# A decode-attention kernel: ScalarE's last seven turns as a hardware loop, exponentials in two halves, last output weights one head a transfer

## The chip, the cores and the metric

One core of a Trainium2 chip runs the kernel. The metric is the device time of one execution in microseconds (us). A program on one core shows no second, slower die to compare with; every run below was judged "fast" by its own spread. Every run was timed in turns with the kernel before on the same chip; the runs were on several chips.

## The reference, cut to what matters

```python
# twice, for A (all 8192 keys) and B (the last 2048 keys): B=4, one query token, 32 heads, 8 kv heads, Dh=128
q = (x @ wq).reshape(B, 1, 32, 128)            # D = 512
scores = einsum("bhqd,bhkd->bhqk", q, k) * 128 ** -0.5
o = einsum("bhqk,bhkd->bhqd", softmax(scores), v)
out = o.reshape(B, 1, 4096) @ wo               # A and B side by side
```

Everything is bfloat16. K and V are read once: 184.56 MB from HBM with the weights.

## The kernel before: the parts that matter here

The work is cut into 20 units (4 of B, then 16 of A: one batch entry, two kv heads), two units to a turn. In unit u, TensorE transposes K of u into PSUM, and VectorE (even groups) and ScalarE (odd groups) copy it to SBUF. TensorE forms the scores, VectorE subtracts the maximum, and ScalarE takes the exponential. One unit later TensorE multiplies by V. K and V have two buffers each, filled by loads that SyncE issues.

```python
def op(eng, fn, waits=(), inc=None, bump=None):
    ...                          # an op with a turn number is emitted once, in a hardware loop
    t = turn[0] if eng == "pe" or (eng == "dve" and turn[0] is not None and turn[0] >= T0P) else None   # T0P = 3

def act_exp(u, h0=0, h1=2):      # h0, h1: which halves of the 1024 columns
    a, b = h0 * NTH * C, h1 * NTH * C
    def fn(act):
        return act.activation(out=PT[:, u % 2, a:b], in_=Dt[:, a:b], func=ACTF.Exp, scale=scale)
    return dict(eng="act", fn=fn, waits=[("sub", u, h1 - 1)] + ([("otr", u - 2)] if u >= 2 else []), ...)

# in kv_load(kind, u): what a load of unit u waits for (the buffer of unit u-2)
w = [("T", tjob_idx[(u - 2, NJ - 1)])] if kind == "K" else [("otr", u - 2)]   # last transpose; scaled output
...                                                                          # SyncE's order: K(u), then V(u-1)

WCH = [3, 2, 2, 1]               # last output weights: heads per transfer
for i, n in enumerate(WCH):      # the last projection, two halves of the columns in two PSUM banks
    for hq in range(h0, h0 + n):
        for hf in range(2):
            ...                  # matmul, waits for ("WL", i)
```

TensorE's ten turns and VectorE's last seven are already hardware loops. A loop of this kernel subtracts what its semaphores gained in each turn (`emit_loop` in the kernel), so no other engine may wait on those semaphores while the loop runs.

Of the kernel before, what the change touches and what calls it, by code (L numbers as in the profile page):

```python
# [14 lines left out]
def bass_concat_heads__gqa_block_cached__sliding_block_cached__decode_kernel(  # L15
# [25 lines left out]
    C = 2 * REP  # L41
    NJ = NT // 8
# [21 lines left out]
    L = NU - 1  # L64
    NTURN = NU // 2
    T0P = 3
# [4 lines left out]
    with ExitStack() as es:  # L71
# [8 lines left out]
        def sm(name):  # L80
# [5 lines left out]
        Wo_sb = sb("Wo_sb", [128, 2, REP, D], BF16)  # L86
# [33 lines left out]
        KTB = [ps("KT%d" % i, 512) for i in range(NBK)]  # L120
        OTB = ps("OT", 512)

        names = ["k0", "k1", "kh", "v0", "v1", "vl0", "vl1", "vl2", "vl3", "wl0", "wl1", "wl2", "wl3", "x0", "x1", "w0", "w1", "wo",
                 "out0", "out1", "out2", "Tq", "Td", "Ta", "S", "PV", "Ed", "Ea", "Eq", "max", "sub", "sum", "rcp", "exp", "otr", "os", "otp",
                 "ocp", "Ef", "fin0", "fin1", "ar1", "SM", "maxc", "pset", "setup", "pm0", "pm1", "oc", "ocB", "mk0", "mk", "mka", "perm", "rq"]
        sems = {n: sm("s_" + n) for n in names}
# [3 lines left out]
        jobs = []  # L130
        bank_last = {}
        follow = {}
        tjob_idx, qp_idx, xt_idx, perm_idx, ot_idx, ol_idx, opj_idx = {}, {}, {}, {}, {}, {}, {}
# [26 lines left out]
        plan = {e: [] for e in ("sp", "pe", "act", "dve", "pool")}  # L160
        turn = [None]

        def op(eng, fn, waits=(), inc=None, bump=None):
            waits = list(waits)
            if not (eng == "pe" and turn[0] is not None):
                waits = [w for w in waits if w is not None]
            t = turn[0] if eng == "pe" or (eng == "dve" and turn[0] is not None and turn[0] >= T0P) else None
            plan[eng].append(dict(fn=fn, waits=waits, inc=inc, turn=t, bump=bump))

        def add(d):  # L170
            op(d["eng"], d["fn"], waits=d["waits"], inc=d["inc"])
# [284 lines left out]
        def act_exp(u, h0=0, h1=2):  # L456
            a, b = h0 * NTH * C, h1 * NTH * C

            def fn(act):
                return act.activation(out=PT[:, u % 2, a:b], in_=Dt[:, a:b], func=ACTF.Exp, scale=scale)  # L460
            return dict(eng="act", fn=fn, waits=[("sub", u, h1 - 1)] + ([("otr", u - 2)] if u >= 2 else []),
                        inc=("exp", u) if h1 == 2 else ("exp", u, h0))

        def dve_sum(u):
            S, n = nseg(u), ncol(u)
# [99 lines left out]
        def dma(dst, src):  # L565
            def fn(e):
                return e.dma_start(out=dst, in_=src)  # L567
            return fn
# [33 lines left out]
        for u in range(NU):  # L602
            turn[0] = tn = u // 2
            odd = u % 2 == 0
            ev = {}
            extra = {}
            at = -1

            def anchored(d):
                extra.setdefault(at, []).append(d)  # L610
            for tok in TOK:
                if tok[0] == "T":
                    ev[tok[1]] = pe_T(u, tok[1])
                    if tok[1] % 2 == 0:
                        at = tok[1]
                elif tok[0] == "S":
                    pe_S(u, tok[1])
                elif tok[0] == "X":
                    if u % 2 == 1:
                        ev["opj"] = pe_job_OPJ(tn)  # L620
                    else:
                        pe_filler(NFILL)
                elif tok[0] == "SM":
                    pe_SM(u - 1)
                else:
                    pe_PV(u - 1, tok[1], waits=[("V", u - 1) if u >= 1 else None] if tok[1] == 0 else [])
                if odd and tok in AFTER:
                    kind = AFTER[tok][0]
                    anchored({"OT": pe_job_OT, "OL": pe_job_OL}[kind](tn))

            if u % 2 == 0 and tn:
                follow[opj_idx[tn - 1]] = tjob_idx[(u, 0)]
            for k in range(0, NJ, 2):
                add(ev[k])
                if k == 10:
                    add(dve_max(u, 0))
                for d in extra.get(k, []):
                    add(d)
            add(dve_max(u, 1))
            if units[u]["P"] == 0:  # L640
                add(dve_maxc(u))
            add(dve_addmask(u))
            if u >= 1:
                add(dve_sum(u - 1))
                add(dve_rcp(u - 1))
            add(dve_submask(u))
            add(dve_sub(u, 0))
            add(dve_sub(u, 1))
            if u >= 1:
                add_norm(u - 1)  # L650
            if u % 2 == 1:
                add(ev["opj"])

            for k in range(1, NJ, 2):
                add(ev[k])
            if u == L:
                add(act_exp(u, 0, 1))
                add(act_exp(u, 1, 2))
            else:
                add(act_exp(u))  # L660

            if u % 2 == 0:
                if tn:
                    op("pool", None, waits=[("ocp", tn - 1)])
                if tn - 1 == T0P + NSEG - 1:
                    op("pool", lambda pool: pool.tensor_copy(out=osb[:, 1, :], in_=oacc[:, :]), inc=("ocB", 0))
                    op("pool", lambda pool: pool.memset(oacc[:, :], 0.0), waits=[("ocB", 0)], inc=("ocB", 1))
                add(pool_otp(tn))
            if u + 1 < NU:
                add(pool_rq(u + 1))  # L670
            add(pool_ar1(u))
            if u >= 1 and units[u - 1]["P"] == 0:
                add(pool_oc(u - 1))
# [14 lines left out]
        for c in range(NC):  # L688
            w = [("VL", vch_of[c])]
# [4 lines left out]
                op("pe", pe_seed, waits=[("ocp", NTURN - 1)])  # L694
            pe_PV(L, c, bank=KTB[0], waits=w)
        add_norm(L, bank=KTB[0])
        WCH = [3, 2, 2, 1]
        h0 = 0
        for i, n in enumerate(WCH):
            for hq in range(h0, h0 + n):  # L700
                for hf in range(2):
                    def lfn(pe, hq=hq, hf=hf):
                        return pe.matmul(out=halves[hf], lhsT=OT_sb[:, 0, NSEG - 1, hq, :], rhs=Wl_sb[:, hq, hf * H2:(hf + 1) * H2],
                                         start=False, stop=(hq == C - 1))
                    op("pe", lfn, waits=[("WL", i), ("otr", L), ("oc", L - 1)], inc=("fin", hf) if hq == C - 1 else None)
            h0 += n
# [4 lines left out]
        def kv_load(kind, u):  # L711
# [6 lines left out]
            if un["P"] == 1:  # L718
                for q in range(NSEG):
                    base = cache[un["b"], 2 * q, SK - W:SK, :]  # L720
                    src = bass.AP(tensor=base.tensor, offset=base.offset, ap=[[TS * DH, 64], [SK * DH, 2], [1, TS * DH]])
                    if kind == "K":
                        w = [("T", tjob_idx[(u - 2, 4 * q + 3)])] if u >= 2 else []
                    else:
                        w = [("otr", u - 2)] if u >= 2 else [("T", tjob_idx[(1, 1)])] if u else [("T", qp_idx[(1, NQP - 1)])]
                    op("sp", dma(buf[:, slot, q * TS:(q + 1) * TS, :], src), waits=w, inc=(kind if q == NSEG - 1 else kind + "h", u, q))
                return
            base = cache[un["b"], 2 * un["gp"], :, :]
            w = [("T", tjob_idx[(u - 2, NJ - 1)])] if kind == "K" else [("otr", u - 2)]
            if kind == "V" and u == L:  # L730
                c0 = 0
                for i, n in enumerate(VCH):
                    t0, t1 = c0 * TC, (c0 + n) * TC
                    src = bass.AP(tensor=base.tensor, offset=base.offset + t0 * DH, ap=[[NT * DH, 128], [1, (t1 - t0) * DH]])
# [17 lines left out]
        for u in range(1, NU + 1):  # L752
            if u < NU:
                kv_load("K", u)
            kv_load("V", u - 1)
            tn = u // 2
            if u % 2 == 0 and tn in pieces:
                P, q = pieces[tn]
                src = WO[P][q * C * DH:(q + 1) * C * DH, :].rearrange("(g p r) n -> p g (r n)", p=128, r=REP)
                op("sp", dma(Wo_sb[:, :, :, :].rearrange("p g r n -> p g (r n)"), src), waits=[("T", tjob_idx[(u, 1)])], inc=("wo", tn))  # L760
            if u == 16:
                op("sp", dma(out[:, 0, D:2 * D], osb[:, 1, :]), waits=[("ocB", 0)], inc=("out", 1))
        h0 = 0
# [31 lines left out]
        def value(key):  # L795
            return values[full(key)]

        def emit(eng_name, eng):
            waited = {}
            for o in plan[eng_name]:  # L800
                for w in o["waits"]:
                    sem, val, _ = value(w)
                    if waited.get(sem.name, 0) >= val:
                        continue
                    eng.wait_ge(sem, val)
                    waited[sem.name] = val
                if o["fn"] is None:
                    continue
                ins = o["fn"](eng)
                if o["inc"] is not None:  # L810
                    sem, val, amt = values[o["inc"]]
                    ins.then_inc(sem, amt)
# [8 lines left out]
        def emit_loop(name, pe, engine):  # L821
# [22 lines left out]
            strides, by_name = {}, {}  # L844
# [27 lines left out]
                    o["w"] = [value(w)[:2] for w in o["waits"]]  # L872
            top0 = {n: max(v for o in turns[0] for s, v in o["w"] if s.name == n) for n in by_name}
            for e in plan:
                assert e == name or not any(value(w)[0].name in by_name for o in plan[e] for w in o["waits"] if w is not None)
            run(ops[:at[0]])
            for n, sem in by_name.items():
                assert strides[n] > 0
# [16 lines left out]

        @block.scalar
        def _(act):
            emit("act", act)

        @block.vector  # L900
        def _(dve):
# [33 lines left out]
```

## Time and profile before

| | kernel before |
|---|---|
| time | 441.33 us median of 3 (441.18 to 441.64) |
| DMA, queue q1 | 98.9% of 16 engines' span, 184.56 MB |
| TensorE / VectorE / ScalarE busy | 83% / 48% / 42% |
| rate from 120 to 400 us | 429 to 431 GB/s |

The page of the kernel before: the span, the busy times, the DMA queues with their packets, megabytes and share of 16 engines, and the chain of waits.

```profile
span 439.6 us, 15816 instructions
PE 366.2 (83%) x7312; PEld 338.0 (77%) x7312; DVE 210.1 (48%) x462; ACT 186.4 (42%) x184; POOL 27.8 (6%) x84
q1 hardware_dynamic: 13088, 184.56, 98.9%
q8 instruction: 8, 0.13, 0.1%
q14 instruction: 6, 0.05, 0.0%
DMA 49%; PE 37%; PEld 8%; issue 3%; SPq 1%; PEldq 0%; DVE 0%; ACT 0%
```

The queue of loads is busy all the time. ScalarE has next to no part in the chain of waits (0% as rounded). q8 and q14 carry the instructions themselves (the page calls both "instruction").

ScalarE's two groups, from the page's costliest groups (busy time, mean of one in ns, then idle time before them and what ended most of it):

```profile
L287 ACT ACTIVATE KT_sb<-KT 128x1024 bf16<-128x1024 bf16 x160 | 163.2, 1024 | 130.6 <-PE KT L278 130.6
L460 ACT ACTIVATE PT<-Dt 128x1024 bf16<-128x1024 f32 (+1 forms) x21 | 21.3, 1017 | 91.8 <-DVE Dt L449 91.8
```

ScalarE waits 222 us in these two groups.

SyncE's queue in the timeline of the kernel before (start, duration, what is issued). K and V come 6.1 us apart in one unit and together in the other:

```profile
187.13 0.34 SPq L567 DMA_DIRECT2D K_sb<-in_A_k_cache_dram  x1
187.58 0.37 SPq L567 DMA_DIRECT2D V_sb<-in_A_v_cache_dram  x1
196.47 0.33 SPq L567 DMA_DIRECT2D K_sb<-in_A_k_cache_dram  x1
202.55 0.33 SPq L567 DMA_DIRECT2D V_sb<-in_A_v_cache_dram  x1
229.16 0.38 SPq L567 DMA_DIRECT2D Wo_sb<-in_B_wo_dram  x1
229.71 0.34 SPq L567 DMA_DIRECT2D K_sb<-in_A_k_cache_dram  x1
```

The last projection in the timeline of the kernel before, some of its 16 matmuls and what follows:

```profile
435.14 0.27 PE L703 MATMUL SA<-Wl_sb,OT_sb 128*4 128x256 bf16 x1
435.77 0.27 PE L703 MATMUL KT<-Wl_sb,OT_sb 128*4 128x256 bf16 x1 [0.36 <-issue]
437.08 0.27 PE L703 MATMUL KT<-Wl_sb,OT_sb 128*4 128x256 bf16 x1
437.28 0.41 DVE L707 CAST osb<-SA 4x256 bf16<-4x256 f32 x1 [2.48 <-PE SA L703]
437.39 0.37 ACT L708 ACTIVATE osb<-KT 4x256 bf16<-4x256 f32 x1 [10.84 <-PE KT L703]
437.79 0.27 ACTq L567 DMA_DIRECT2D out_dram<-osb  x1
```

Matmuls of this kind start 0.11 us apart. Between the third and the fourth there are 0.63 us.

The trace also records 16 landings of every transfer of 128 partitions, without naming an engine. I take each for one of the 16 DMA engines that the page counts; 16 packets of q1 are in flight for 91% of the time from 60 to 400 us. The tables in plain fences in this text are worked out from such records, and from those of single packets. Times are from the span's start:

```
kernel before, transfer landed (its slowest engine)   slowest - second   - median   - first
K, 142.6 us                                                0.04 us       0.27 us    2.13 us
V, 216.7 us                                                0.96          1.22       3.10
V, 423.9 us                                                0.53          1.26       2.77
last weights, 436.51 us                                    0.46          1.10       2.45
```

The engines do not keep step: from 153 to 434 us the slowest and the fastest are 2.7 to 3.1 us apart. They do not even out either: the slowest stays 0.94 to 1.00 us behind the second from 153 to 382 us, and 0.4 to 0.6 us from 392 us to the end. The last weights are complete only when the slowest has landed, at 436.51 us, 1.10 us after the median.

### The profile page before, as it was taken

To read this page: it belongs to the slowest core of one execution; us is meant where nothing else is said; L and a number is where in the kernel's file an instruction comes from. 1 tells how busy PE (TensorE), PEld (TensorE's weight loads), DVE (VectorE), ACT (ScalarE), POOL (GpSimd) and SP (SyncE) were. 2 spreads that over 40 slices of the span, in tenths; PEclk is the share of its full clock that TensorE was granted. 3 is DMA by queue.
4 is the path that set the end of the run, shared out by engine and by line. 5 is a ranking of instruction groups with operands and counts; after the bars stand their busy time and mean duration, and the time that the engine had idled before them with its cause. 6 is when DMAs were issued, how large, how long until landed. Compare 5 with 4: busy or idle time off the path is not lost.

```text
span 439.6 us, 15816 instructions
## 1 busy us (share of the span) xinstructions
PE 366.2 (83%) x7312; PEld 338.0 (77%) x7312; DVE 210.1 (48%) x462; ACT 186.4 (42%) x184; POOL 27.8 (6%) x84
## 2 busy tenths in 40 slices
PE   0158998998997949895989698969878896989986
PEld 0158897997996949795979688968878795979965
DVE  0034455654663634463446346625643563556641
ACT  1004473473562615370635253434534361635630
POOL 6100000000000000000000000000100000000000
PEclk9999999999999988998899799969997999899999
DMA  8999999999999999999999999999999999999995
GB/s 338 427 413 421 418 417 421 423 441 409 444 429 436 418 438 429 429 427 429 432 438 420 433 444 422 437 432 429 413 446 435 429 430 429 432 427 411 447 403 211
DMA packets 13190, 184.77 MB, mean 420 GB/s; under 512 B 1348, under 2 KB 2424, under 8 KB 4472
## 3 DMA queue, kind: packets, MB, share of 16 engines
q1 hardware_dynamic: 13088, 184.56, 98.9%
q8 instruction: 8, 0.13, 0.1%
q14 instruction: 6, 0.05, 0.0%
q0 software_dynamic: 64, 0.02, 0.0%
q10 hardware_dynamic: 24, 0.01, 0.0%
HBM read 184.56 MB, written 0.01 MB: 420 GB/s over the span
## 4 chain that ended last, share of the span: by engine, by line
DMA 49%; PE 37%; PEld 8%; issue 3%; SPq 1%; PEldq 0%; DVE 0%; ACT 0%
DMA K_sb<-in_A_k_cache_dram 37%; PE KT L278 21%; DMA K_sb<-in_B_k_cache_dram 7%; PE OT L325 6%; DMA Wl_sb<-in_A_wo_dram 5%; PEld KT L278 3%; PE SA L309 3%; PE SB L309 3%; PE KT L387 2%; PEld OT L325 1%; SPq L567 1%; PEld SA L309 1%; PEld SB L309 1%; PE SA L337 1%; PE KT L261 0%
## 5 line engine op out<-in xcount | busy, mean ns | idle before, releaser
L278 PE MATMUL KT<-identf,K_sb 128*128 128x128 f32 x1280 | 208.4, 297 | 45.3 <-DMA K_sb<-in_A_k_cache_dram 32.9
L287 ACT ACTIVATE KT_sb<-KT 128x1024 bf16<-128x1024 bf16 x160 | 163.2, 1024 | 130.6 <-PE KT L278 130.6
L278 PEld LDWEIGHTS KT<-identf,K_sb 128*128 128x128 f32 x1280 | 147.6, 149 | 50.8 <-DMA K_sb<-in_A_k_cache_dram 34.1
L286 DVE COPY KT_sb<-KT 128x512 int32<-128x512 int32 x160 | 110.5, 690 | 121.8 <-PE KT L278 120.4
L325 PE MATMUL OT<-PT,V_sb 128*128 128x64 bf16 x2560 | 78.1, 193 | 2.1 <-DMA V_sb<-in_A_v_cache_dram 1.2
L325 PEld LDWEIGHTS OT<-PT,V_sb 128*128 128x128 bf16 x2560 | 75.9, 98 | 2.3 <-DMA V_sb<-in_A_v_cache_dram 1.3
L460 ACT ACTIVATE PT<-Dt 128x1024 bf16<-128x1024 f32 (+1 forms) x21 | 21.3, 1017 | 91.8 <-DVE Dt L449 91.8
L309 PEld LDWEIGHTS SA<-RQc,KT_sb 128*128 128x128 bf16 x1280 | 57.2, 98 | 2.5
L309 PEld LDWEIGHTS SB<-RQc,KT_sb 128*128 128x128 bf16 x1280 | 50.5, 97 | 7.9 <-issue 4.4
L309 PE MATMUL SA<-RQc,KT_sb 128*128 128x16 bf16 x1280 | 56.5, 170 | 0.0
L309 PE MATMUL SB<-RQc,KT_sb 128*128 128x16 bf16 x1280 | 52.8, 170 | 0.0
L411 DVE TENSOR_REDUCE M<-SB 128x8 f32<-128x512 f32 (+1 forms) x20 | 13.8, 692 | 50.3 <-PE SB L309 50.3
L432 POOL PARTITION_ALL_REDUCE MB<-M1m x20 | 7.7, 387 | 335.7 <-DVE M1m L425 335.7
L387 PE MATMUL KT<-Wo_sb,OL 128*4 128x512 bf16 x80 | 18.9, 379 | 0.0
L197 PE MATMUL KT<-ident,x_sb 4*128 4x4 bf16 x8 | 0.6, 170 | 19.5 <-POOL identf L529 19.5
L197 PEld LDWEIGHTS KT<-ident,x_sb 4*128 4x128 bf16 x8 | 0.4, 113 | 19.6 <-issue 19.6
L449 DVE TENSOR_TENSOR Dt<-SA,MBm 128x512 f32<-128x512 f32 x20 | 13.8, 691 | 0.7
L411 DVE TENSOR_REDUCE M<-SA 128x8 f32<-128x512 f32 (+1 forms) x20 | 13.6, 681 | 0.0
L449 DVE TENSOR_TENSOR Dt<-SB,MBm 128x512 f32<-128x512 f32 x20 | 13.6, 681 | 0.0
L337 PE MATMUL SA<-PT,onesb 128*128 128x64 bf16 x336 | 13.2, 192 | 0.0
L387 PEld LDWEIGHTS KT<-Wo_sb,OL 128*4 128x4 bf16 x80 | 6.0, 84 | 8.1
L337 PEld LDWEIGHTS SA<-PT,onesb 128*128 128x128 bf16 x336 | 11.1, 97 | 0.0
(72 smaller groups left out, 125.4 us busy)
## 6 DMA issues: line engine op xcount, KB each, us to landing
K_sb<-in_A_k_cache_dram SPq DMA_DIRECT2D x15, 4096.0 KB, 24.5
V_sb<-in_A_v_cache_dram SPq DMA_DIRECT2D x15, 4096.0 KB, 29.5
K_sb<-in_B_k_cache_dram SPq DMA_DIRECT2D x16, 1024.0 KB, 22.1
V_sb<-in_B_v_cache_dram SPq DMA_DIRECT2D x16, 1024.0 KB, 19.0
V_sb<-in_B_wq_dram SPq DMA_DIRECT2D x1, 4096.0 KB, 12.3
V_sb<-in_A_wq_dram SPq DMA_DIRECT2D x1, 4096.0 KB, 21.7
Wo_sb<-in_B_wo_dram SPq DMA_DIRECT2D x4, 1024.0 KB, 10.2
K_sb<-in_A_k_cache_dram SPq DMA_DIRECT2D x2, 2048.0 KB, 17.3
```

The source lines that it names most:

```text
L278: ins = pe.transpose(out=bkf[:, pi * 128:(pi + 1) * 128], in_=K_sbf[:, slot, t0:t0 + 2, :].rearrange("p t d -> p (t d)"), identity=identf[ ...
L286: return e.tensor_copy(out=KT_sb.bitcast(I32)[:, tj % NKT, :], in_=bkf.bitcast(I32)[:, :])
L287: return e.activation(out=KT_sb[:, tj % NKT, :], in_=bk[:, :], func=ACTF.Copy)
L309: ins = pe.matmul(out=stb[:, t % NTH * C:(t % NTH + 2) * C], lhsT=ktv[:, pi, :, e], rhs=RQc[:, u % 2, t // TS, e, :], start=(e == 0), stop ...
L325: ins = pe.matmul(out=otb[:, s * NW:s * NW + w], lhsT=V_sb[:, slot, t, :], rhs=PT[:, slot, t * C:t * C + w], start=(j == 0), stop=(j == n ...
L337: ins = pe.matmul(out=SA[u % 2][:, s * NW:(s + 1) * NW], lhsT=onesb[:, :], rhs=PT[:, u % 2, c0:c0 + NW], start=(i == 0), stop=(i == n - 1))
L387: ins = pe.matmul(out=bk[0:Bn, 0:D], lhsT=OL[:, i // REP, i % REP, :], rhs=Wo_sb[:, i // REP, i % REP, :], start=(i == 0), stop=(i == C - 1))
L411: return dve.tensor_reduce(out=M1[:, h * n:(h + 1) * n].rearrange("p (s h) -> p s h", h=C), in_=bank[:, :].rearrange("p (s j h) -> p s h j ...
L432: return pool.partition_all_reduce(MB[:, 0:n], M1m[:, 0:n], channels=128, reduce_op=ReduceOp.max)
L449: return dve.tensor_tensor(out=Dt[:, h * NTH * C:(h + 1) * NTH * C].rearrange("p (s j h) -> p s j h", s=Sh, h=C), in0=bank[:, :].rearrange ...
L460: return act.activation(out=PT[:, u % 2, a:b], in_=Dt[:, a:b], func=ACTF.Exp, scale=scale)
L567: return e.dma_start(out=dst, in_=src)
```

## The change

The intent: ScalarE's program becomes a loop as the others' are (fewer instructions to load), the exponential of the first half starts before the second half is subtracted, and the last projection starts with one head's weights. Since a loop's semaphores may not be waited on by others, the loads of K and of the output weights get waits on VectorE's results instead of on the transposes that ScalarE copies. The diff, with only the list of semaphore names left out:

```diff
-            t = turn[0] if eng == "pe" or (eng == "dve" and turn[0] is not None and turn[0] >= T0P) else None
+            t = turn[0] if eng == "pe" or (eng in ("dve", "act") and turn[0] is not None and turn[0] >= T0P) else None
@@ act_exp
-            return dict(eng="act", fn=fn, waits=[("sub", u, h1 - 1)] + ([("otr", u - 2)] if u >= 2 else []),
-                        inc=("exp", u) if h1 == 2 else ("exp", u, h0))
+            return dict(eng="act", fn=fn, waits=[("sub", u, h1 - 1)], inc=("exp", u) if h1 == 2 else ("exp", u, h0))
@@ each unit
-            if u == L:
-                add(act_exp(u, 0, 1))
-                add(act_exp(u, 1, 2))
-            else:
-                add(act_exp(u))
+            add(act_exp(u, 0, 1))
+            add(act_exp(u, 1, 2))
@@ last projection
-        WCH = [3, 2, 2, 1]
+        WCH = [1] * C
-                for hf in range(2):
+                for hf in (1, 0):
@@ kv_load
-            w = [("T", tjob_idx[(u - 2, NJ - 1)])] if kind == "K" else [("otr", u - 2)]
+            w = [("otr", u - 2)] if kind == "V" else [("otr", u - 3)] if u >= 2 * T0P else [("T", tjob_idx[(u - 2, NJ - 1)])]
@@ output weights of the earlier pieces
-                op("sp", dma(Wo_sb...), waits=[("T", tjob_idx[(u, 1)])], inc=("wo", tn))
+                op("sp", dma(Wo_sb...), waits=[("ocp", tn - 1)], inc=("wo", tn))
@@ emit_loop: waits of turns before the loop are allowed
-                assert e == name or not any(value(w)[0].name in by_name for o in plan[e] for w in o["waits"] if w is not None)
+                assert e == name or not any(value(w)[0].name in by_name for o in plan[e] for w in o["waits"] if w is not None
+                                                  and not (name == "act" and w[0] == "T" and (jobs[w[1]]["turn"] or 0) < T0P))
@@ block.scalar
-            emit("act", act)
+            emit_loop("act", act, mybir.EngineType.Activation)
```

More of the change, by code (lines that the diff above doesn't have):

```diff
@@ L121, in bass_concat_heads__gqa_block_cached__sliding_block_cached__decode_kernel @@
         OTB = ps("OT", 512)
-        names = ["k0", "k1", "kh", "v0", "v1", "vl0", "vl1", "vl2", "vl3", "wl0", "wl1", "wl2", "wl3", "x0", "x1", "w0", "w1", "wo",
+        names = ["k0", "k1", "kh", "v0", "v1", "vl0", "vl1", "vl2", "vl3", "wl0", "wl1", "wl2", "wl3", "wl4", "wl5", "wl6", "wl7", "x0", "x1", "w0", "w1", "wo",
                  "out0", "out1", "out2", "Tq", "Td", "Ta", "S", "PV", "Ed", "Ea", "Eq", "max", "sub", "sum", "rcp", "exp", "otr", "os", "otp",
@@ L759, in bass_concat_heads__gqa_block_cached__sliding_block_cached__decode_kernel @@
                 src = WO[P][q * C * DH:(q + 1) * C * DH, :].rearrange("(g p r) n -> p g (r n)", p=128, r=REP)
-                op("sp", dma(Wo_sb[:, :, :, :].rearrange("p g r n -> p g (r n)"), src), waits=[("T", tjob_idx[(u, 1)])], inc=("wo", tn))
+                op("sp", dma(Wo_sb[:, :, :, :].rearrange("p g r n -> p g (r n)"), src), waits=[("ocp", tn - 1)], inc=("wo", tn))
             if u == 16:
```

## The prediction

> **What bounds the kernel now.** The DMA engines. The page gives 184.77 MB in a span of 439.6 us, 420 GB/s over the span, queue q1 busy 98.9% of the 16 engines' time; in the windows view the rate is 427 to 431 GB/s from 60 to 400 us. [...] ScalarE is busy 42%, TensorE 83% (it waits 32.9 us for A's K tiles). The chain of waits is 49% DMA.
>
> The end is set by the slowest of the 16 DMA engines. The trace's landing records (16 per transfer) show it about 0.95 us behind the second from 153 us on (0.5 from 392 us), after one 8 KB instruction packet at 150.6 us: the data packet next to it took 1.88 us, not 1.22. [...]q14 here carries those packets. By count of instructions that one is VectorE's, which the change does not touch. ScalarE's own (I take the one at 249.6 us, after 114 of its 209 instructions) hit the fastest engine.
>
> **What the change does.**
> 1. ScalarE loop: its code shrinks by about 100 instructions, so one 8 KB packet (0.31 us of one engine) should vanish. It adds 7 branches. TensorE's loop shows 1.3 to 1.4 us of "issue" at each turn's end; ScalarE's falls where it waits for TensorE anyway (130.6 us of such waits). Gain: 0 to 0.5 us, only if the packet's engine matters; I expect 0.1.
> 2. Exponentials in halves: 1.02 us becomes two, 1.23 us together (read at the last unit, which already does it); the first starts some 0.6 us earlier. About 4 us more ScalarE work in all, none on the chain.
> 3. K from unit 6 on waits for the output of unit u-3 instead of the last transpose of u-2: about 6.1 us later (issues at 196.5 and 202.6 us, now together). The queue still holds 14 us of data then (the previous V lands at 216.7). The output weights wait for the earlier projection's eviction, about 1.5 us earlier, which frees the queue for the next K. The smallest queue, 6.9 us at 229.2 us, grows to about 8.5. No time on the chain.
> 4. Last weights: 4 transfers become 8 of 128 KB, same 1 KB packets, 4 more issues of 0.45 us on SyncE, hidden under the queue. The last head lands at 436.5 us as before; the last multiplications end at 437.35, 2.3 us before the end. TensorE pauses 0.65 us after the third of the 16 multiplications, apparently for instructions, which I expect to remain.
> 5. ScalarE's half first: ScalarE's copy (0.37 us) instead of VectorE's (0.41) starts first: under 0.1 us.
>
> **Predicted time:** 441.1 us, 80% range 440.4 to 441.8. Chances: faster by over 2% 0.01, within 2% 0.98, slower 0.01.
>
> **What would show it.** DMA share of q1 stays at 98 to 99%; one q14 packet fewer; K issues of A together with V's in the queue's timeline; ScalarE busy about 190 us; exp group x40 near 0.62 us; last weights landing within 0.5 us of 436.5; the gap of the slowest DMA engine to the second unchanged.
>
> **What would make it wrong.** [...] The later K issues leaving the engines dry (rate below 420 GB/s in slices after 120 us). SyncE held so long on the eight small issues that the last weights come late. Or the vanished packet having been on the slowest engine: 0.5 us faster.

441.33 us for the kernel before, less the 0.1 us of the loop and under 0.1 us of ScalarE's half, comes to about the 441.1 us predicted, and the rate in it is the trace's own, 427 to 431 GB/s.

## The result, and the profile after

The changed kernel takes 441.14 us (median of 6 runs, 440.98 to 441.39), the kernel before 441.36 us (6 runs) beside it. The ratio is 0.9995, with a 95% interval of 0.9982 to 1.0008: the same. A ratio here is the mean time of one kernel's fast runs over that of the other's of the same rounds, so it is not quite the ratio of the medians quoted.

The page of the changed kernel, the lines that answer to those shown of before:

```profile
span 439.6 us, 15842 instructions
PE 365.9 (83%) x7302; PEld 338.4 (77%) x7312; DVE 210.1 (48%) x462; ACT 189.7 (43%) x203; POOL 27.8 (6%) x84
q1 hardware_dynamic: 13152, 184.56, 98.9%
q8 instruction: 8, 0.13, 0.1%
q14 instruction: 5, 0.04, 0.0%
DMA 46%; PE 45%; PEld 4%; issue 2%; DVE 1%; SPq 1%; PEldq 0%
```

Bytes, share and span are unchanged; one q14 packet is gone. The shares of the chain moved between DMA and PE while the span did not, so nothing can be read from that move.

ScalarE's groups of the changed kernel:

```profile
L287 ACT ACTIVATE KT_sb<-KT 128x1024 bf16<-128x1024 bf16 x160 | 163.3, 1024 | 138.0 <-PE KT L278 138.0
L460 ACT ACTIVATE PT<-Dt 128x512 bf16<-128x512 f32 x40 | 24.6, 630 | 80.4 <-DVE Dt L449 80.4
```

The halves did what they were meant to do: ScalarE waits 11.4 us less for the subtraction (80.4 for 91.8), about 0.57 us a unit. It spends 3.3 us more on the exponentials and waits 7.4 us more for TensorE. The gain turned into a longer wait behind the next unit's transposes.

SyncE's queue after, at the same place:

```profile
186.79 0.33 SPq L566 DMA_DIRECT2D K_sb<-in_A_k_cache_dram  x1
187.22 0.38 SPq L566 DMA_DIRECT2D V_sb<-in_A_v_cache_dram  x1
203.62 0.33 SPq L566 DMA_DIRECT2D K_sb<-in_A_k_cache_dram  x1
204.05 0.38 SPq L566 DMA_DIRECT2D V_sb<-in_A_v_cache_dram  x1
227.44 0.38 SPq L566 DMA_DIRECT2D Wo_sb<-in_B_wo_dram  x1
228.00 0.33 SPq L566 DMA_DIRECT2D K_sb<-in_A_k_cache_dram  x1
```

K is issued 7.1 us later at 203.62, together with V. By the landings, the V issued before it lands at 216.7 us, so 13.1 us of loads are still queued then. When the next output weights (Wo) are issued at 227.44 it is 8.7 us (the V of 204.05 lands at 236.14); the same point of the kernel before has 7.0 us. The shortest stretch between 60 and 395 us is 8.5 us, at 186.23. The queue never runs dry.

The last projection after:

```profile
435.09 0.27 PE L699 MATMUL KT<-Wl_sb,OT_sb 128*4 128x256 bf16 x1
435.86 0.27 PE L699 MATMUL SA<-Wl_sb,OT_sb 128*4 128x256 bf16 x1 [0.50 <-issue]
437.17 0.27 PE L699 MATMUL SA<-Wl_sb,OT_sb 128*4 128x256 bf16 x1
437.37 0.37 ACT L704 ACTIVATE osb<-KT 4x256 bf16<-4x256 f32 x1 [10.84 <-PE KT L699]
437.48 0.41 DVE L703 CAST osb<-SA 4x256 bf16<-4x256 f32 x1 [2.71 <-PE SA L699]
437.92 0.28 SPq L566 DMA_DIRECT2D out_dram<-osb  x1
```

The first head's weights landed at 434.19 us instead of 434.88, and the last at 436.49 instead of 436.51. But the product with V is ready only at about 434.8 us (OT_sb), and the pause after the third matmul is still there, 0.77 us from start to start. So the last matmul starts at 437.17 instead of 437.08.

The instruction packets that the trace records after the span's start:

```
            q14, 8 KB each, at us                              q8, 16 KB each, at us
before      53.2  137.6  150.6  188.7  249.6  388.0            25.4 ... 70.4 (7 of them), 433.3
after       53.2  111.5  152.3  189.8  250.1    -              25.9 ... 70.4 (7 of them), 433.3
```

The packet that vanished is the one at 388.0 us. In the kernel before the six q14 packets took 0.31 to 0.32 us each, and beside each of the last five a 32 KB data packet took 1.57 to 1.88 us; the median of such packets is 1.22.

### The profile page after: what moved, and what is told of

Its sections match the earlier page's. It is cut to its first block, busy times and chain, and to the rows that moved or that the text cites. A ratio compares the mean times of both kernels' runs of the same rounds, so it can differ in the third digit from the quotient of the medians.

```text
span 439.6 us, 15842 instructions
## 1 busy us (share of the span) xinstructions
PE 365.9 (83%) x7302; PEld 338.4 (77%) x7312; DVE 210.1 (48%) x462; ACT 189.7 (43%) x203; POOL 27.8 (6%) x84
## 3 DMA queue, kind: packets, MB, share of 16 engines
q1 hardware_dynamic: 13152, 184.56, 98.9%
## 4 chain that ended last, share of the span: by engine, by line
DMA 46%; PE 45%; PEld 4%; issue 2%; DVE 1%; SPq 1%; PEldq 0%
DMA K_sb<-in_A_k_cache_dram 35%; PE KT L278 23%; PE OT L325 9%; DMA K_sb<-in_B_k_cache_dram 7%; DMA V_sb<-in_A_v_cache_dram 4%; PE SA L309 4%; PE SB L309 4%; PE KT L387 3%; PEld KT L278 2%; SPq L566 1%; PE SA L337 1%; PE KT L325 1%; DVE oacc L395 1%; PEld OT L325 1%; PEld SA L309 1%
## 5 line engine op out<-in xcount | busy, mean ns | idle before, releaser
L287 ACT ACTIVATE KT_sb<-KT 128x1024 bf16<-128x1024 bf16 x160 | 163.3, 1024 | 138.0 <-PE KT L278 138.0
L460 ACT ACTIVATE PT<-Dt 128x512 bf16<-128x512 f32 x40 | 24.6, 630 | 80.4 <-DVE Dt L449 80.4
```

The source lines that it names most:

```text
L287: return e.activation(out=KT_sb[:, tj % NKT, :], in_=bk[:, :], func=ACTF.Copy)
```

## The experiments

The theory: the DMA engines' work sets the time, the slowest of the 16 sets the end, and ScalarE is not on the chain. The rivals: the loop gains something that the late K loads take back; the finer weights gain something that the loop takes back; ScalarE's own work counts; or total bandwidth counts, not the slowest engine. Changed kernel below means the 441.14 us version; it was timed in other rounds, so the ratios given are to the kernel before, which ran beside each.

### One part undone: the loop

```diff
-            t = ... (eng in ("dve", "act") and turn[0] is not None and turn[0] >= T0P) ...
+            t = ... (eng == "dve" and turn[0] is not None and turn[0] >= T0P) ...
-            emit_loop("act", act, mybir.EngineType.Activation)
+            emit("act", act)
```

> The changed kernel with ScalarE's program unrolled again (halved exponentials, new waits and eight weight transfers kept). Theory (the 16 DMA engines' work is fixed, and the slowest of them sets the end; ScalarE is off the chain): 441.2 us, within 0.3 us of the changed kernel (441.1); one more 8 KB instruction packet on q14 (6 instead of 5 after the start), late in the run. Rival (the loop was a gain of its own, hidden by a loss of the late K loads): 0.5 us or more above the changed kernel.

Measured: 441.12 us, ratio to before 0.9991 (0.9977 to 1.0004). The extra q14 packet is back, at 371.2 us. In all three kernels here that unroll ScalarE the lag of the slowest DMA engine behind the second shrinks after that packet, by 0.3 to 0.5 us; in the looped ones with nothing else added it changes by less than 0.1:

```
slowest engine minus second        at 258 us      at 424 us
before (unrolled)                   0.95 us        0.53 us
late K loads alone (unrolled)       0.94           0.61
changed, unrolled again             0.79           0.26
changed (looped)                    0.73           0.71
changed, weights in 4 (looped)      1.02           0.93
```

The shrinking says that some engine came closer to the slowest; it does not say which. For that, line up the 16 landings of a transfer before the packet with those of one after it, and let one engine be delayed and the other 15 not. With the late K loads alone it is the ninth-slowest engine, 1.28 us ahead of the slowest, that loses 0.68 us and so becomes the second (the other 15 then agree within 0.04 us; if the second-slowest had been hit they would be off by up to 0.16). In the kernel before it is the fifth-slowest, 1.18 us ahead, and it also loses 0.68 us (0.01 against 0.08). In the unrolled run the fit does not decide.

So ScalarE's packet falls on an engine near the middle of the 16. It costs that engine 0.68 us: its own 0.31, and 0.37 because the 32 KB data packet beside it takes 1.59 us instead of 1.22. That makes it the second-slowest engine, with 0.3 to 0.6 us still to spare. Taking the packet away therefore moves the end by nothing.

### One part alone: the late K loads

```diff
 (kernel before)
-            w = [("T", tjob_idx[(u - 2, NJ - 1)])] if kind == "K" else [("otr", u - 2)]
+            w = [("otr", u - 2)] if kind == "V" else [("otr", u - 3)] if u >= 2 * T0P else [("T", ...)]
-                op("sp", dma(Wo_sb...), waits=[("T", tjob_idx[(u, 1)])], inc=("wo", tn))
+                op("sp", dma(Wo_sb...), waits=[("ocp", tn - 1)], inc=("wo", tn))
```

> The kernel before with only the waits of the K loads and of the output weights moved as the change has them. Theory: the queue never runs dry, so 441.3 us, within 0.2 us of before, q1's share still 98 to 99%, though A's K tiles are issued 5 to 7 us later every second unit. Rival (the late K loads cost what the rest gains): 0.5 us or more above before.

Measured: 441.25 us, ratio 0.9993 (0.9979 to 1.0006), q1 at 99.0%. The late loads cost nothing, so there is no hidden loss for the loop to make up.

### One part undone: the finer weights

```diff
-        WCH = [1] * C
+        WCH = [3, 2, 2, 1]
-                for hf in (1, 0):
+                for hf in range(2):
```

> The changed kernel with the last output weights in 4 transfers again (3, 2, 2, 1 heads) and VectorE's half first. Theory: the last weights land at the same time (436.5 us of the span), the multiplications are held by TensorE's own pause of 0.8 us and end at the same time: within 0.2 us of the changed kernel. Rival (the finer transfers are a gain hidden by the loop's cost): 0.3 us or more above it.

Measured: 441.17 us, ratio 0.9990 (0.9977 to 1.0004). The time is the changed kernel's within 0.03 us. In this profile the pause was shorter (0.22 us from start to start instead of 0.11), so its length varies by execution; I had expected it to be 0.8 us each time.

### Twice the exponentials

```diff
             def fn(act):
+                act.activation(out=scr[:, a:b], in_=Dt[:, a:b], func=ACTF.Exp, scale=scale)
                 return act.activation(out=PT[:, u % 2, a:b], in_=Dt[:, a:b], func=ACTF.Exp, scale=scale)
```

> The changed kernel with every exponential computed a second time into a scratch tile: about 24.6 us more ScalarE work (189.7 to 214 us busy). Theory: ScalarE is off the chain, so 441.2 us, within 0.4 us of the changed kernel; ScalarE waits less for TensorE instead. Rival (ScalarE's work is on the chain at the units' ends): up to 1.26 us a unit, 5 to 25 us slower.

Measured: 441.04 us, ratio 0.9989 (0.9976 to 1.0003). ScalarE's groups in this run:

```profile
L288 ACT ACTIVATE KT_sb<-KT 128x1024 bf16<-128x1024 bf16 x160 | 163.2, 1024 | 120.1 <-PE KT L279 120.0
L461 ACT ACTIVATE scr<-Dt 128x512 bf16<-128x512 f32 x40 | 24.9, 622 | 80.4 <-DVE Dt L450 80.4
L462 ACT ACTIVATE PT<-Dt 128x512 bf16<-128x512 f32 x40 | 24.5, 613 | 0.0
```

The extra work shows in the groups (24.9 us more), and the wait for TensorE fell from 138.0 to 120.1 us. (The page's total is 208.9 us and the groups of ScalarE add up to 214.5, so 5.6 us of instructions overlap there.) ScalarE could do 24.9 us more work, against the 3.3 us that the change added, at no cost.

### Half of one V left out (a wrong result)

```diff
+            if kind == "V" and u == 10:     # load only the first half of this V
+                src = bass.AP(tensor=base.tensor, offset=base.offset, ap=[[NT * DH, 128], [1, NTH * DH]])
+                op("sp", dma(buf[:, slot, 0:NTH, :]..., src), inc=(kind, u, 0)); return
```

> The changed kernel with half of one unit's V (2 MB of unit 10) not loaded; the result is wrong on purpose. Theory (the DMA engines' work sets the time): 2.10 MB less at 431 GB/s, so 4.9 us less: 436.3 us. Rival (TensorE, busy 83%, or its waits set the time): less than 1 us.

Measured: 436.5 us, ratio 0.9883 (0.9867 to 0.9900), the result wrong. 2.10 MB less saved 4.6 us against the changed kernel, and 4.95 against the kernel before beside it. Bytes are what the time is made of. Whether the engines themselves or the memory behind them set the 431 GB/s, this run does not tell.

### The same bytes on fewer engines

A load that nobody reads, issued in mid-run into an unused tile `scr`, in four shapes:

```diff
+            if u == 10:
+                xb = KC[0][0, 0, :, :]
+                op("sp", dma(scr[0:P, 0:N], bass.AP(tensor=xb.tensor, offset=xb.offset, ap=[[NT * DH, P], [1, N]])), inc=("xtra",))
 # P, N = 128, 4352 | 68, 2048 | 17, 2048 | 64, 2048
```

> The changed kernel with one more load in mid-run that nobody reads: 128 partitions of 8.5 KB, 1.11 MB, 68 KB on each of the 16 DMA engines. Both theories: 1.11 MB at 431 GB/s, 2.6 us more, 443.7 us.

> The same, but 68 partitions of 4 KB, 0.28 MB[...]. Theory (the slowest engine sets the end[...]): 2.4 to 2.7 us more, 443.7 us, as if all 16 had it, and the lag of the slowest engine over the median grows from 1.4 us to about 3.9. Rival (the total bandwidth is what counts, the engines even each other out): 0.28 MB at 431 GB/s, 0.65 us more.

> The same with 17 partitions of 4 KB[...]. Theory: 2.5 us minus the slack of engine 0, which no record names: 0 (engine 0 is the fastest, 2.8 us ahead at the end) to 2.5 us more (it is the slowest). Rival (total bandwidth): 0.07 MB, 0.16 us more.

> The changed kernel with an extra load of 64 partitions of 4 KB, 0.26 MB, that nobody reads[...]. The run with 68 partitions cost 5 us, not the 2.5 of its four engines' own bytes, and packets beside it took 1.9 us instead of 1.2. If what an engine moves is all that counts: 0.26 MB at 431 GB/s, 0.6 us more (441.8 us). [...]

| extra load | bytes | per engine used | time | over the changed kernel | slowest minus median, 217 us / end |
|---|---|---|---|---|---|
| 128 partitions | 1.11 MB | 68 KB on 16 | 443.83 us | 2.7 us | 1.37 / 1.32 us |
| 68 partitions | 0.28 MB | 68 KB on 4 | 446.19 us | 5.0 us | 1.54 / 4.62 us |
| 17 partitions | 0.07 MB | 68 KB on 1 | 442.89 us | 1.75 us | 1.18 / 2.33 us |
| 64 partitions | 0.26 MB | 16 KB on 16 (assumed) | 443.93 us | 2.8 us | 1.49 / 1.74 us |

Against the kernel before, timed in the same rounds, the four cost 2.4, 4.7, 1.4 and 2.6 us. All are under 2%, but every interval excludes 1.

The engines in the third column are read from landings. In the traces of both kernels a transfer of 128 partitions lands 16 times and one of 4 partitions 4 times, apart from one record at the issue; so read, the 68-partition load shows four landings and the 17-partition load one. For 64 partitions I have no such count: 16 engines is my assumption. It fits that this load held up the median landing nearly as much as the slowest (2.0 and 2.3 us). The expectations assumed 68 KB on each of four engines, the slowest among them, and 68 KB on one. Which engine took a load, no record tells; "engine 0" in the expectation is only a name for that one. That the slowest would be among the four was my guess from the 4-partition output transfer issued at 352 us: its last landing, 363.08 us, came 0.2 us after the slowest of the full transfer beside it, 362.89. That both use the same four engines is not shown.

Three things follow. First, total bandwidth as the only limit falls: 0.28 MB at 431 GB/s is 0.65 us, and it cost 5.0. Second, the slowest engine counts. The loads of 68 and of 64 partitions have nearly the same bytes; the one packed onto four engines cost 2.3 us more, and only there did the slowest engine fall 3.1 us further behind the median, up to the end. Third, my number for the 68-partition load was half of what it cost, and the 64-partition load shows why the simple theory is incomplete: with, on that assumption, only 16 KB on each engine it held up the slowest engine by 2.3 us, from the landing at 217 us to the one that is at 258 us in the changed kernel, and the median by 2.0. The 68-partition load held up the median nearly as much, 1.9 us, and the slowest by 5.1. So about 2 us of its cost reached the median engine too, and about 3.2 more the four that it used (my estimate by their own bytes is 2.6: 68 KB at a sixteenth of 431 GB/s). The 17-partition load fits (1.75 us, where bandwidth alone gives 0.16), but its range of 0 to 2.5 us left little to miss. Beside the 64-partition load, 4 KB packets took up to 0.30 us instead of 0.16 and 32 KB packets up to 1.85 us instead of 1.22 (medians of one us). The windows of 236 to 246 us (busy time of each engine, granted clock, DMA share, GB/s) show it, first for the changed kernel, then with 68, then with 64 partitions:

```profile
236.00:246.00 10.00, 8.24 (x224) 7.79 (x221) 5.29 (x14) 4.29 (x5) 0.79 (x3) 1.00 1.02 439
```

```profile
236.00:246.00 10.00, 8.84 (x233) 8.38 (x231) 5.89 (x14) 4.56 (x6) 0.79 (x3) 1.00 1.02 351
```

```profile
236.00:246.00 10.00, 8.66 (x230) 8.12 (x228) 5.63 (x14) 4.31 (x6) 0.79 (x3) 1.00 1.03 384
```

The engines are as busy as ever (1.02 and 1.03 of their time) and move less. By bytes alone the 64-partition load would cost 0.6 us (0.26 MB at 431 GB/s); measured were 2.8. The 17-partition load slowed 32 KB packets too (to 1.42 us); the 128-partition load, with the most bytes, did not (1.22 throughout). The cause stays open.

### Moving the pause out of the last projection

The pause looked like a wait for instructions. The changed kernel has eight 16 KB instruction packets on q8; the last one comes at 433.3 us, 2.5 us before the fourth matmul starts, the one after the pause (435.86). From one of the seven early packets to the next the trace has 212 to 369 TensorE instructions, 273 on average, so I supposed a piece of TensorE's program behind each packet and an edge between two pieces at the pause. Two runs pad TensorE's setup with small matmuls (two instructions each): 118 should shift that edge out of the last projection, and 128, as a control, should bring the next one to the same place. That 128 matmuls make just one piece was my assumption. No trace shows it (the mean of 273 instructions is 137 matmuls).

```diff
+        def pe_pad(pe):
+            for _ in range(118):     # 128 in the control
+                ins = pe.matmul(out=SB[:, 0:4], lhsT=ident[:, :], rhs=ident[:, 0:4], start=True, stop=True)
+            return ins
         for P in (1, 0):
+            if P == 0:
+                op("pe", pe_pad, waits=[("setup",)])
             pe_job_xT(P)
```

> The changed kernel with 118 small dummy matmuls on TensorE in the setup, where it waits for the first K anyway. They shift TensorE's program by 236 instructions against its 16 KB instruction packets[...], so that the packet now read in the middle of the last 16 matmuls is needed some 115 matmuls earlier, during the wait for the last V. Theory (the 0.8 us pause in the last projection is that packet, and it holds the end): the pause is gone, the last projection ends about 0.4 us after the last weights land (436.5 us) instead of 1.0: 440.7 us, 0.3 to 0.5 under the changed kernel. Rival (the pause is the wait for the weights, whatever reports it): within 0.1 us of it.

> Control: the same with 128 dummy matmuls[...]. Theory: the pause of 0.7 to 0.8 us is back in the last 16 matmuls, 441.1 us as the changed kernel. Rival (the padding itself, by the moved start, changes the time): as the run with 118.

Measured: 441.44 us (ratio 1.0003, 0.9989 to 1.0016) and 441.37 us (1.0001, 0.9988 to 1.0015). I missed. With 118 the pause was gone, but the matmuls then came in pairs at the pace of the weights, and the weights came late:

```profile
435.17 0.27 PE L706 MATMUL SA<-Wl_sb,OT_sb 128*4 128x256 bf16 x1
435.39 0.27 PE L706 MATMUL KT<-Wl_sb,OT_sb 128*4 128x256 bf16 x1
435.50 0.27 PE L706 MATMUL SA<-Wl_sb,OT_sb 128*4 128x256 bf16 x1
435.69 0.27 PE L706 MATMUL KT<-Wl_sb,OT_sb 128*4 128x256 bf16 x1
```

```
                          q8 packets late in the run      last weights landed   slowest minus median at 424 us / there
changed kernel            433.3                           436.49 us             1.38 / 1.22 us
padded by 118             433.1, 436.8                    437.33                1.44 / 1.93
padded by 128 (control)   433.0, 436.6                    437.29                1.34 / 2.03
8-matmul sums (below)     433.5                           436.81                1.59 / 1.45
```

Both padded runs show two q8 packets more, one in the first 80 us and one at the end. Only the first can be put down to the padding: a packet at 436.7 us also stands in the changed kernel with the weights in 4 transfers, which has no padding. Between the first and the second of the last eight transfers the slowest engine loses 0.5 and 0.7 us on the median. That would fit the packet at 433 us falling on that engine now, but no record names the engine. The control did not separate what it was meant to, since its pause is hidden behind the late weights too.

The traces say more about the pause than these two runs. In the changed kernel, its variants and the kernel before the pause comes after the third matmul; in the eight of their profiles that show one, of 0.22 to 0.77 us, the fourth matmul starts 2.4 to 2.6 us after the start of the q8 packet before it, however long the pause is. In three of the runs with an extra load TensorE came there later than that, and there was no pause. This fits a wait for that packet; no run isolates it. Wherever there is no pause, padded runs included, the last matmul ends 0.42 us after the last weights land; with it, 0.45 to 0.95 us. So in the changed kernel the pause, and not the last weights, holds the last half microsecond.

### An attempt at a better version: a shorter TensorE program

```diff
-                    n = TS * C // NW
+                    n = TS * C // (2 * NW)
-                        c0 = s * TS * C + i * NW
-                        ins = pe.matmul(out=SA[u % 2][:, s * NW:(s + 1) * NW], ..., rhs=PT[:, u % 2, c0:c0 + NW],
+                        c0 = s * TS * C + i * 2 * NW
+                        ins = pe.matmul(out=SA[u % 2][:, s * 2 * NW:(s + 1) * 2 * NW], ..., rhs=PT[:, u % 2, c0:c0 + 2 * NW],
```

(VectorE's sum then reads 512 columns instead of 256.)

> The changed kernel with the sums of the exponentials as 8 matmuls of 128 columns instead of 16 of 64 in each unit (an attempt at a better version). TensorE's program shrinks by 48 instructions, so the edge of the instruction packet that now falls after the third of the last 16 matmuls moves past the last one, without a further packet in the run (the padded runs had one more, at 433 us, and the slowest DMA engine lost 0.6 us to it in the last weights). Theory (pause and packet hold the end together): no pause, last weights at 436.5 us of the span, last matmul about 0.4 us earlier than the changed kernel, 440.7 us. Rival: the packet then falls on the slowest engine, as in the padded runs, and the weights come 0.8 us late: 441.4 us. VectorE's sum takes 0.27 us longer a unit, off the chain.

Measured: 441.04 us (440.61 to 441.14), before 441.47 beside it, ratio 0.9988 (0.9975 to 1.0002). The pause is gone and no packet was added; these are the third, the fourth and the last matmul:

```profile
435.40 0.27 PE L699 MATMUL KT<-Wl_sb,OT_sb 128*4 128x256 bf16 x1
435.50 0.27 PE L699 MATMUL SA<-Wl_sb,OT_sb 128*4 128x256 bf16 x1
436.96 0.27 PE L699 MATMUL SA<-Wl_sb,OT_sb 128*4 128x256 bf16 x1
```

The last matmul ends 0.42 us after the last weights (437.23 and 436.81); in the changed kernel it is 0.95 us (437.44 and 436.49). In the profiled execution the weights happened to land 0.3 us later, which ate most of it. The median is 0.1 us under the changed kernel, in different rounds, and the interval of the ratio contains 1: a better version than either is not shown.

## Why the prediction was right, point by point

- The time: 441.1 predicted, 441.14 measured. The reason given, that the DMA engines' fixed work sets the time and the slowest engine the end, held in the main: bytes taken away saved 4.6 us, doubled exponentials cost nothing, and 0.28 MB that landed four times cost 5.0 us, where 0.26 MB in 64 partitions cost 2.8. It does not hold for the last 0.5 us, which TensorE's pause adds after the slowest engine is done.
- Halved exponentials off the chain: right (0.62 us predicted for one, 0.63 measured; ScalarE 190 predicted, 189.7 measured).
- Late K loads: right. The queue held 13.1 us (14 predicted) and, at its shortest, 8.5 us (8.5 predicted). K came 7.1 us later (6.1 predicted).
- The loop: one packet fewer, as predicted (five on q14 after the start, six before), and none added for the turns of its loop. But the step "ScalarE's own (I take the one at 249.6 us ...) hit the fastest engine" was wrong. The packet at 249.6 us did hit the fastest engine, but it was not ScalarE's: it is still there at 250.1 us after the change, after 314 of VectorE's instructions both times. The packet that left was the one at 388.0 us, and it had fallen on an engine near the middle of the 16. Its cost was mis-sized too: 0.68 us of that engine, not 0.31. The gain of nothing was right for another reason than the one given, and partly by luck: an engine 1.18 us ahead of the slowest could lose 0.68 us; had the packet fallen on the slowest, that one would, by my estimate, have been later by as much.
- "The gap of the slowest DMA engine to the second unchanged" was wrong in the same step: at 424 us it was 0.53 us before and 0.71 after, since no packet late in the run moves another engine up behind the slowest any more.
- The last weights: right, 436.5 us in both; and the pause stayed, as predicted (0.63 us from start to start, then 0.77).
- ScalarE's half first: "under 0.1 us" of gain did not appear. Its transfer of the result left at 437.77 us instead of 437.79, but SyncE's left at 437.92 instead of 437.72.

Left open: whether the 0.2 us by which the changed kernel's median lies under before is real. Most of its variants show it too (0.2 to 0.4 us), but the interval of each contains 1. Not tested either: what time would be saved without the q14 packet at about 151 us. It comes at the same count of VectorE's instructions (181 to 183) in the seven traces that I counted, and in all 14 profiles the lag of the slowest engine behind the median grew by 0.7 to 1.0 us between 143 and 217 us. A VectorE program short enough to avoid it was not made.

## What to carry to other kernels

When the DMA queue is busy 99% of the time (here q1, 98.9%), ask of every change whether it takes bytes away (2.10 MB less saved 4.6 us) or relieves the slowest of the 16 DMA engines. Work on an engine that waits half its time may change nothing but its wait: 24.9 us more of it on ScalarE left the time at 441.04 us. The landing records of a few large transfers show how far the slowest engine is behind (at 216.7 us 0.96 us behind the second, 1.22 behind the median). What falls on another engine need not move the end: here 0.68 us on an engine 1.18 us ahead of the slowest did not make it the last. When a gap between two ranks changes, line up all 16 landings before saying which engine was hit. An experiment near a program's end can move instruction packets as well as the thing under test (both padded runs showed two more on q8, one of them put down to the padding), so count them before and after.
